# Keys loaded head dimension first, their parts written straight into place; queries loaded to both halves of the partitions

## The chip, the cores and the metric

The kernel runs on one core of a Trainium2 chip. The metric is the device time of one execution in microseconds (us), taken as the median of several runs. The core has five engines that run side by side, each through its own list of instructions, in the order in which the program wrote it: TensorE (PE, matrix products), VectorE (DVE), ScalarE (ACT), GpSimd (POOL) and SyncE (SP). SP and ACT also issue the DMA transfers here.

## The reference, cut to what matters

Attention of 4 batches, 8 heads, 768 positions and head dimension 64 is followed by a bilinear feed-forward layer. The positions form 24 blocks of 32. A query block sees its neighbours, the first and the last block, and three sampled blocks; the first and the last query block see all.

```python
scores = scale * np.matmul(q, k.transpose(0, 1, 3, 2))
mask = np.abs(blk_i - blk_j) <= window
mask = mask | (blk_i == 0) | (blk_j == 0) | (blk_i == n_blocks - 1) | (blk_j == n_blocks - 1)
for qb in range(n_blocks):
    for kb in sampled_blocks[qb]:
        mask[qb * block:(qb + 1) * block, kb * block:(kb + 1) * block] = True
scores = np.where(mask, scores, -1000000000.0)
attn = exp(scores - max) / (sum + 1e-09)
attn_out = np.matmul(attn, v)
x = attn_out.transpose(0, 2, 1, 3).reshape(B * S, H * D)
return ((x @ w_a) * (x @ w_b)) @ w_out
```

The weights are 512 by 1536 (`w_a`, `w_b`) and 1536 by 512 (`w_out`) and reach the chip as 64-bit floats.

## The kernel before

To keep the accuracy of 32 bits on a 16-bit array, each operand is scaled by a power of two and split into a high part (the value in float16) and a low part (what is left, in float16). The second product of the feed-forward layer uses 32-bit parts instead.

**Keys.** `keys(b, g)` loads the keys of two heads of batch `b` (group `g` of four) as 128 positions by 768 numbers (L471). ACT takes the largest absolute value (L481), POOL reduces it over the partitions (L370), DVE makes a scale of it in three small operations (L373, L376, L379). ACT writes the high part (L486), DVE the low part beside it (L487), both into a tile `ks`, of which there are three, shared with the value passes. Positions now lie on the partitions, but the product needs the head dimension there, so SP issues a DMA transpose of `ks` into `keysT` (L495): high part on partitions 0 to 63, low part on 64 to 127. `keysT[1]` and the raw-key buffers serve as landing place for the weights until all of these are unpacked (`w_freed`), and `keysT[b % 2]` is used in turn by the batches (`k_free`).

**Queries.** `queries(cc)` loads 256 positions of all heads, head dimension on partitions 0 to 63 (L633), takes the largest value (L641), and writes the high part (L646, ACT) and the low part (L648, DVE). SP then copies each part to the other half of the partitions (L672, two copies a chunk), so that `QT[:, 0]` holds high over low and `QT[:, 1]` low over high. A product of `QT[:, 0]` and of `QT[:, 1]` with a key column then adds all four combinations.

**Attention of a block (a "unit").** POOL gathers the 8 key blocks into `KG` (L572 to L577); PE writes the mask (L857) and the scores (L756); DVE takes maxima (L872, L875); ACT exponentiates (L882); DVE or ACT write the high part of the probabilities `hl` (L777 or L774) and DVE the low part (L781); SP transposes `hl` to `pt` by DMA (L904); SP loads the value rows `VG` (L607 to L612) from a copy of the split values in DRAM (`vd`, written at L531); PE multiplies (L800); ACT and DVE split the result into `xT` (L1044, L1047). The first and last block take the same way over all keys (L959, L974, L999).

**Feed-forward.** Per chunk of 256 positions: 12 first products `ab` (L1082, 24 matmuls each), ACT and DVE multiply them (L1114, L1117) and split the result (L1139, L1142), and PE makes the second products (L1170 to L1172). The weights are unpacked by DVE from the 64-bit words (L703, L706, L709, three operations a tile), measured and split (L723, L730, L731, L736, L737), interleaved with the attention of the first batch. The second chunk's products are parked in DRAM (L1120) and read back (L1133).

**What sets the order.** All of this is written as flows (Python generators) that ask for an engine, a duration and a rank. `Plan.run` simulates the engines and the DMA with these durations and issues the instruction that could start earliest, weighed by rank. So a changed step changes the order of all engines' lists. The lists are then fixed: an instruction that waits holds up everything behind it on its engine.

Of the kernel before, what the change touches and what calls it, by code (L numbers as in the profile page):

```python
# [224 lines left out]
def act(ns, fn):  # L225
    return [Way("ACT", ns, fn)]
# [16 lines left out]
def kernel(  # L243
# [83 lines left out]
    k_ready = [Event(NG) for _ in range(B)]  # L327
# [5 lines left out]
    q_ready = [Event(3) for _ in range(NC)]  # L333
# [49 lines left out]
    def make_tables():  # L383
# [14 lines left out]
        def load():  # L398
            nc.scalar.dma_start(
                one.rearrange("p a b -> p (a b)"),  # L400
                sampled_blocks.bitcast(I32).rearrange("(o a) b -> o (a b)", o=1),
            )
            nc.scalar.dma_start(
                sb.rearrange("p a b -> p (a b)"), sampled_blocks.bitcast(I32)
            )
            nc.scalar.dma_start(cb, c_blocks)

        yield [Way("ACT", 300, load, 250)]
# [59 lines left out]
    def keys(b, g):  # L468
        yield from gate(first_of[b] - GATE_KV)
        raw, freed = yield from raw_tile(b, g, 0)  # L470
        yield load_way(1000, lambda: nc.scalar.dma_start(raw, k[b, g]))  # L471
        if g + 1 < NG:
            plan.start(keys(b, g + 1), first_of[b] - LEAD_K)
        elif b > 0:
            plan.start(values(b, 0), first_of[b] - LEAD_V)
        t = raw.rearrange("p (t d) -> p t d", d=D)
        done = yield from take("ks", KS_BUFS)
        ks = work.tile([P, 2 * NT, P], F16, tag="ks", name=f"ks{b}_{g}", bufs=KS_BUFS)
        at = at_k + b * NG + g
        s = scale[:, at : at + 1]  # L480
        yield act(1020, lambda: nc.scalar.activation(  # L481
            ks[:, :, :D], t, AF.Abs, accum_out=bound[:, at : at + 1]
        ))
        end = yield from set_scale(slice(at, at + 1), FLOOR_QK)
        k_scale[b].fire(end)
        yield act(930, lambda: nc.scalar.activation(ks[:, :, :D], t, AF.Copy, scale=s))  # L486
        end = yield dve(1070, lambda: nc.vector.scalar_tensor_tensor(  # L487
            ks[:, :, D:], t, s, ks[:, :, :D], ALU.mult, ALU.subtract
        ))
        freed.fire(end)  # L490
        if b == 1:
            yield w_freed
        if b >= 2:
            yield k_free[b - 2]
        end = yield sp(1700, 2200, lambda: nc.sync.dma_start_transpose(  # L495
            keysT[b % 2][:, 2 * g : 2 * g + 2, :].rearrange("p h (t s) -> p (h t) s", s=P),
            ks.rearrange("p t d -> p (t d)"),
        ))
        done.fire(end)
        k_ready[b].fire(end)  # L500
# [125 lines left out]
    def queries(cc):  # L626
# [6 lines left out]
        yield load_way(1400, lambda: nc.scalar.dma_start(t[:D], q[b, c]))  # L633
        if cc + 1 < NC:
# [5 lines left out]
        high, low_ = QT[cc][:D, 0], QT[cc][:D, 1]  # L640
        yield act(2080, lambda: nc.scalar.activation(  # L641
            high, t[:D], AF.Abs, accum_out=bound[:D, at : at + 1]
        ))
        yield from set_scale(slice(at, at + 1), FLOOR_QK)
        s = scale[:D, at : at + 1]
        end = yield act(1890, lambda: nc.scalar.activation(high, t[:D], AF.Copy, scale=s))  # L646
        plan.start(turn_queries(cc, 0), u0 - LEAD_Q, end)
        end = yield dve(2350, lambda: nc.vector.scalar_tensor_tensor(  # L648
            low_, t[:D], s, high, ALU.mult, ALU.subtract
        ))  # L650
        freed.fire(end)
        plan.start(turn_queries(cc, 1), u0 - LEAD_Q, end)
# [15 lines left out]
        q_ready[cc].fire(end)  # L668

    def turn_queries(cc, a):  # L670

        end = yield sp(650, 700, lambda: nc.sync.dma_start(  # L672
            QT[cc][D:, 1 - a], QT[cc][:D, a]
        ))
        q_ready[cc].fire(end)
# [550 lines left out]
def _laid_out(name, a):  # L1226
# [10 lines left out]
    elif name in ("k", "v"):  # L1237
# [3 lines left out]
        a = a.transpose((0, 1, 4, 2, 3, 5) if name == "k" else (0, 1, 4, 3, 2, 5))  # L1241
# [35 lines left out]
```

## Time and profile before

| | us |
|---|---|
| three runs | 924.38, 928.32, 932.67 |
| median | 928.32 |
| span of the profiled execution | 931.3 |

The profiled execution's own time is not given apart from its span; the span lies 3.0 us above the median and inside the range of the three runs. In the rows of the profile, "busy" is time in which an engine worked, a bracket such as [1.86 <-DMA VG<-vd] is the idle time ahead of an instruction and what ended it, and SPq or ACTq is the engine's own queue of DMA issues. Over the span PE is busy 85%, DVE 63%, ACT 49% and POOL 19%. The page's picture in 40 slices shows PE nearly idle for the first tenth and nearly full in the last fifth:

```profile
PE   0134696689869988899989889899999999999998
DVE  3999998977557866765766665645774735432222
DMA  9969999599687699985766984636764706431000
```

### The profile page before, as it was taken

The page shows a single profiled execution, that of the slowest core. Times are in us where ns is not written, and L with a number is a line of the kernel's source. Part 1 is how long each engine was busy: PE and PEld are TensorE (multiplying, and loading weights), DVE is VectorE, ACT ScalarE, POOL GpSimd, SP SyncE. Part 2 cuts the span into 40 slices and gives each one's busy share as a digit, 9 for nine tenths or more (in the row PEclk, how much of TensorE's full clock was granted, in tenths as well). Part 3 has the DMA queues.
Part 4 walks back from the last instruction along what each step waited for, and adds up shares of the span by engine and source line. Part 5 has one row for each costly group of instructions (what it writes and reads, how often), then busy time and mean ns, then how long its engine had stood idle before and what let it go on. Part 6 is the DMA issues. An engine that isn't in the chain of part 4 may idle for free.

```text
span 931.3 us, 23890 instructions
## 1 busy us (share of the span) xinstructions
PE 788.2 (85%) x9024; PEld 629.5 (68%) x9024; DVE 582.6 (63%) x1603; ACT 454.6 (49%) x1087; POOL 176.3 (19%) x416
## 2 busy tenths in 40 slices
PE   0134696689869988899989889899999999999998
PEld 0123584477647776678777777788777778888886
DVE  3999998977557866765766665645774735432222
ACT  4665665566445556554555464434654433332222
POOL 0550232321013421200332320000441300000000
PEclk9999798899989998999999999999999999999999
DMA  9969999599687699985766984636764706431000
GB/s 249 323 165 255 260 242 249 139 172 244 178 201 163 144 203 188 210 172 131 150 155 165 209 164 141 146 79 152 165 141 120 132 1 149 103 97 47 23 1 23
DMA packets 212222, 145.51 MB, mean 156 GB/s; under 512 B 152841, under 2 KB 180490, under 8 KB 211338
## 3 DMA queue, kind: packets, MB, share of 16 engines
q1 hardware_dynamic: 201280, 106.22, 52.4%
q10 hardware_dynamic: 10826, 37.76, 13.7%
q8 instruction: 71, 1.16, 0.5%
q14 instruction: 45, 0.37, 0.1%
HBM read 87.82 MB, written 14.16 MB: 110 GB/s over the span
## 4 chain that ended last, share of the span: by engine, by line
PE 49%; DMA 20%; DVE 18%; ACT 5%; issue 4%; SPq 3%; POOL 1%; ACTq 0%; POOLq 0%; DVEq 0%
PE ab L1082 26%; DMA pt<-hl 12%; PE o L1170 5%; PE o L1172 5%; PE o L1171 4%; PE av L800 4%; DMA keysT<-ks 4%; DVE hl L781 4%; PE s L756 3%; DVE hl L777 2%; DVE xT L1047 1%; DMA VG<-vd 1%; DVE low L872 1%; ACT sm L882 1%; ACT xT L1044 1%
## 5 line engine op out<-in xcount | busy, mean ns | idle before, releaser
L1082 PE MATMUL ab<-xT,wab 128*128 128x256 f16 x3456 | 412.3, 277 | 7.7 <-DVE xT L1047 3.8
L1082 PEld LDWEIGHTS <-wab 128*128 128x128 f16 x3456 | 333.0, 99 | 81.7 <-issue 40.3
L1170 PE MATMUL o<-woh,gh 128*128 128x512 f32 x288 | 128.3, 445 | 13.5 <-ACT gh L1139 13.3
L1114 ACT ACTIVATE a<-ab,f 128x256 f32<-128x256 f32 x144 | 67.8, 471 | 142.5 <-PE ab L1082 131.7
L1117 DVE TENSOR_TENSOR a<-a,ab 128x256 f32<-128x256 f32 x144 | 60.2, 418 | 122.7 <-ACT a L1114 121.8
L882 ACT ACTIVATE sm<-s,low,cq 128x256 f32<-128x256 f32 x176 | 98.1, 560 | 79.1 <-DVE hl L781 43.6
L800 PE MATMUL av<-pt,VG 128*128 128x64 f16 x2688 | 105.7, 196 | 33.9 <-DMA VG<-vd 20.4
L800 PEld LDWEIGHTS <-VG 128*128 128x128 f16 x2688 | 96.3, 100 | 53.2 <-issue 38.5
L1172 PE MATMUL o<-woh,gl 128*128 128x512 f32 x288 | 117.1, 407 | 1.6 <-DVE gl L1142 1.6
L1171 PE MATMUL o<-wol,gh 128*128 128x512 f32 x288 | 115.3, 400 | 0.0
L572 POOL COPY KG<-keysT 128x384 int32<-128x384 int32 x88 | 53.4, 607 | 322.6 <-PE s L756 292.8
L781 DVE SCALAR_TENSOR_TENSOR hl<-sm,den,hl 128x256 f16<-128x256 f32 (+1 forms) x208 | 106.1, 517 | 9.8 <-ACT hl L774 7.6
L577 POOL COPY KG<-keysT 128x128 int32 x264 | 98.1, 409 | 41.3 <-POOL KG L572 27.2
L777 DVE TENSOR_SCALAR hl<-sm,den 128x256 f16<-128x256 f32 (+1 forms) x150 | 57.2, 382 | 59.1 <-DMA pt<-hl 59.0
L1139 ACT CAST gh<-a 128x256 fp32r<-128x256 f32 x132 | 53.2, 403 | 64.2 <-DVE a L1117 63.2
L1170 PEld LDWEIGHTS o<-woh,gh 128*128 128x128 f32 x288 | 55.2, 192 | 33.3 <-ACT gh L1139 16.7
L756 PE MATMUL s<-KG,QT 128*32 128x256 f16 x1408 | 61.1, 299 | 19.4 <-POOL KG L577 19.4
L1142 DVE TENSOR_TENSOR gl<-a,gh 128x256 fp32r<-128x256 f32 x132 | 57.5, 436 | 30.8 <-ACT gh L1139 29.2
L1047 DVE SCALAR_TENSOR_TENSOR xT<-av,xT 64x256 f16<-64x256 f32 x96 | 40.4, 421 | 54.5 <-ACT xT L1044 53.4
L857 PE MATMUL s<-mrows,ident 128*32 128x192 bf16 (+1 forms) x352 | 26.1, 285 | 56.2 <-ACT sm L882 29.6
L756 PEld LDWEIGHTS <-QT 128*32 128x32 f16 x1664 | 45.0, 103 | 34.9 <-issue 29.9
L1172 PEld LDWEIGHTS o<-woh,gl 128*128 128x128 f32 x288 | 55.6, 193 | 18.2 <-DVE gl L1142 5.5
(93 smaller groups left out, 744.5 us busy)
## 6 DMA issues: line engine op xcount, KB each, us to landing
VG<-vd SPq DMA_DIRECT2D x284, 64.0 KB, 2.4
VG<-vd SPq DMA_DIRECT2D x88, 192.0 KB, 3.1
VG<-vd SPq DMA_DIRECT2D x32, 384.0 KB, 3.5
q<-in_q_dram ACTq DMA_DIRECT2D x12, 512.0 KB, 5.5
QT<-QT SPq DMA_DIRECT2D x24, 256.0 KB, 3.9
vd<-vs SPq DMA_DIRECT2D x16, 384.0 KB, 4.6
out_dram<-ou SPq DMA_DIRECT2D x24, 256.0 KB, 3.4
stage<-in_k_dram ACTq DMA_DIRECT2D x12, 384.0 KB, 3.7
```

The lines of the kernel that those rows point to most:

```text
L577: nc.gpsimd.tensor_copy(to[:, :, (5 + r) * w : (6 + r) * w], of[:, :, bass.ds(at, w)])
L756: mm(to[h * BLK : (h + 1) * BLK], q_block(cc, i, 4 * hq + h, a), rhs(4 * hq + h), start=(first and a == 0), stop=(a == 1), skip_group_chec ...
L777: Way("DVE", 227 + n * 0.49, lambda: nc.vector.tensor_scalar(hi, sm, over, None, ALU.mult), 0, X_HIGH),
L781: t = yield dve(221 + n * 1.03, lambda: nc.vector.scalar_tensor_tensor(lo, sm, over, hi, ALU.mult, ALU.subtract))
L800: mm(av[:, g, i % 2, :], w, pt[:, y, cols], start=(i % 2 == 0 and g == 0 and first and n + m == 0), stop=(last and n == len(terms) - 1 and ...
L882: t = yield act(750, lambda hq=hq: nc.scalar.activation(sm[:, hq], ps[:, hq], AF.Exp, bias=low[:, at, hq, 0:1], scale=cq[:, cc, hq : hq + ...
L1082: mm(ab[:, i, :], wab[:, f, i, part, kt, :], xc[:, kt, a, :], start=(i == 0 and kt == 0 and part + a == 0), stop=(kt == KT - 1 and a == 1) ...
L1114: yield act(470, lambda: nc.scalar.activation(a_sb, ab[:, 0, :], AF.Copy, scale=fb[:, f : f + 1]))
L1117: t = yield dve(420, lambda: nc.vector.tensor_mul(a_sb, a_sb, ab[:, 1, :]))
L1170: mm(po, gh[:, js], woh[:, f, :], start=(f == 0), stop=False)
L1171: mm(po, gh[:, js], wol[:, f, :], start=False, stop=False)
L1172: mm(po, gl[:, js], woh[:, f, :], start=False, stop=(f == NF - 1))
```

## The change

The host lays the keys out with the head dimension first: a group's tile is now 2 heads by 64 dimensions on the partitions, and 768 positions along each. The scale is made as before, but the absolute pass writes to a spare tile that is free again at once. Then `key_parts(b, g, x)` runs for each of the two heads. The high part is made by ACT or DVE, whichever the planner finds first, from the 64 partitions of the head straight into `keysT`; DVE writes the low part into the other 64 partitions of the same columns. For the first head of a group the high part lies on partitions 0 to 63, for the second on 64 to 127. The DMA transposes are gone. A pass now works on 64 partitions and 768 columns, so there are two where there was one.

The queries are loaded twice, to partitions 0 to 63 and 64 to 127, and the passes run over 128 partitions at the same column count. `QT[:, 0]` is now the high part on both halves, `QT[:, 1]` the low part; the sum over both is the same four combinations. The copies by SP are gone. The three small loads of the block table move from ACT's queue to SP's.

```diff
-    k_ready = [Event(NG) for _ in range(B)]
+    k_ready = [Event(H) for _ in range(B)]
-    q_ready = [Event(3) for _ in range(NC)]
+    q_ready = [Event(2) for _ in range(NC)]
...
-            nc.scalar.dma_start(cb, c_blocks)
+            nc.sync.dma_start(cb, c_blocks)
...
-        yield act(930, lambda: nc.scalar.activation(ks[:, :, :D], t, AF.Copy, scale=s))
-        end = yield dve(1070, lambda: nc.vector.scalar_tensor_tensor(
-            ks[:, :, D:], t, s, ks[:, :, :D], ALU.mult, ALU.subtract
-        ))
-        freed.fire(end)
         if b == 1:
             yield w_freed
         if b >= 2:
             yield k_free[b - 2]
-        end = yield sp(1700, 2200, lambda: nc.sync.dma_start_transpose(
-            keysT[b % 2][:, 2 * g : 2 * g + 2, :].rearrange("p h (t s) -> p (h t) s", s=P),
-            ks.rearrange("p t d -> p (t d)"),
-        ))
-        done.fire(end)
+        left = Event(2)
+        for x in range(2):
+            plan.start(key_parts(b, g, x, raw, at, left, freed), first_of[b] - LEAD_K, end)
+
+    def key_parts(b, g, x, raw, at, left, freed):
+
+        mine, other = slice(64 * x, 64 * x + 64), slice(64 - 64 * x, 128 - 64 * x)
+        to = keysT[b % 2]
+        s = scale[mine, at : at + 1]
+        h = 2 * g + x
+        yield [
+            Way("ACT", 930, lambda: nc.scalar.activation(
+                to[mine, h], raw[mine], AF.Copy, scale=s
+            )),
+            Way("DVE", 600, lambda: nc.vector.tensor_scalar(
+                to[mine, h], raw[mine], s, None, ALU.mult
+            )),
+        ]
+        end = yield dve(1050, lambda: nc.vector.scalar_tensor_tensor(
+            to[other, h], raw[mine], s, to[mine, h], ALU.mult, ALU.subtract
+        ))
...
-        yield load_way(1400, lambda: nc.scalar.dma_start(t[:D], q[b, c]))
+        def load():
+            for half in range(2):
+                nc.scalar.dma_start(t[half * D : (half + 1) * D], q[b, c])
+
+        yield [Way("LOAD", 950, load, 2600, 1)]
...
-    def turn_queries(cc, a):
-
-        end = yield sp(650, 700, lambda: nc.sync.dma_start(
-            QT[cc][D:, 1 - a], QT[cc][:D, a]
-        ))
-        q_ready[cc].fire(end)
```

PE's list has the same matmuls, and at the first product of each feed-forward chunk the same attention stands ahead of it but for one unit in places. What moves is on the other engines.

On DVE at the start of the program, before (L487 writes the low part of a group's keys, L411 is the first operation on the block table):

```order
L373 TENSOR_SCALAR power<-power 128x1
L487 SCALAR_TENSOR_TENSOR ks_0_113<-wab,scale,ks_0_113 128x12x64
L376 TENSOR_SCALAR rscale<-power 128x1
L487 SCALAR_TENSOR_TENSOR ks_1_115<-wab,scale,ks_1_115 128x12x64
L379 RECIPROCAL scale<-rscale 128x1
L487 SCALAR_TENSOR_TENSOR ks_2_117<-wab,scale,ks_2_117 128x12x64
L411 TENSOR_SCALAR mrow<-mrow 1x72
```

On DVE at the same place now (L504 is the high part of one head's keys, L508 its low part, L555 the reduction of the values' bound):

```order
L379 RECIPROCAL scale<-rscale 128x1
L504 TENSOR_SCALAR keysT_77<-wab,scale 64x768 x2
L379 RECIPROCAL scale<-rscale 128x1
L504 TENSOR_SCALAR keysT_77<-wab,scale 64x768
L508 SCALAR_TENSOR_TENSOR keysT_77<-wab,scale,keysT_77 64x768 x6
L555 TENSOR_REDUCE bound<-bound_v 128x1
L373 TENSOR_SCALAR power<-power 128x1
L411 TENSOR_SCALAR mrow<-mrow 1x72
```

All eight low parts and five of the eight high parts now stand on DVE ahead of the table; ACT has the other three high parts.

On ACT at the start, before (L506 loads values, L486 is a group's high part, L633 loads the first chunk of queries, L399 the table):

```order
L506 DMA wab<-in_v_dram 128x768
L486 ACTIVATE ks_0_113<-wab,scale 128x12x64
L506 DMA wab<-in_v_dram 128x768
L486 ACTIVATE ks_1_115<-wab,scale 128x12x64
L633 DMA q_109<-in_q_dram 64x2048
L486 ACTIVATE ks_2_117<-wab,scale 128x12x64
L399 DMA mrow<-in_sampled_blocks_dram 1x144
```

On ACT at the same place now (L520 loads values, L479 is the keys' absolute pass, L528 the values', L650 loads the queries):

```order
L520 DMA wab<-in_v_dram 128x768
L479 ACTIVATE ks_3_120,bound<-wab 128x768
L520 DMA wab<-in_v_dram 128x768
L528 ACTIVATE va_0_123,bound_v<-wab 128x768
L650 DMA q_109<-in_q_dram 64x2048 x2
L528 ACTIVATE va_1_128,bound_v<-wab 128x768
L528 ACTIVATE va_2_135,bound_v<-wab 128x768
```

The queries' load, now two transfers, stands behind the first value's absolute pass instead of behind the second key's high part.

On SP where the keys of the second batch (b = 1) are made, before (L904 turns probabilities, L1120 parks a product, L495 turns keys, L607 begins the value rows of a unit):

```order
L904 DMA_TRANSPOSE pt_2645<-hl_2601 128x8x128
L1120 DMA parked_g<-a_0_2583 128x256
L495 DMA_TRANSPOSE keysT_78<-ks_0_2501 128x12x128
L1120 DMA parked_g<-a_1_2640 128x256
L495 DMA_TRANSPOSE keysT_78<-ks_1_2515 128x12x128
L1120 DMA parked_g<-a_2_2700 128x256
L1120 DMA parked_g<-a_3_2736 128x256
L495 DMA_TRANSPOSE keysT_78<-ks_2_2517 128x12x128
L495 DMA_TRANSPOSE keysT_78<-ks_3_2675 128x12x128
L607 DMA VG_86<-vd_79 96x1024
```

On SP at the same place now (L1131 parks, L915 turns probabilities, L621 begins the value rows):

```order
L1131 DMA parked_g<-a_0_2583 128x256
L915 DMA_TRANSPOSE pt_2659<-hl_2593 128x8x128
L1131 DMA parked_g<-a_1_2632 128x256
L1131 DMA parked_g<-a_2_2694 128x256
L621 DMA VG_86<-vd_79 96x1024
L566 TENSOR_LOAD offs
```

Nothing of the keys stands ahead of the value rows any more. In exchange 8 low parts and 3 high parts stand within 22 rows of DVE's list there (5 high parts are on ACT), where 4 low parts stood within 27. Over the whole program DVE has 32 low parts of keys where it had 16, 19 high parts of keys where it had none, and 122 high parts of probabilities where it had 150; ACT has 86 of these where it had 58, and 13 high parts of keys where it had 16.

More of the change, by code (lines that the diff above doesn't have):

```diff
@@ L398, in load @@
         def load():
-            nc.scalar.dma_start(
+            nc.sync.dma_start(
                 one.rearrange("p a b -> p (a b)"),
@@ L402, in load @@
             )
-            nc.scalar.dma_start(
+            nc.sync.dma_start(
                 sb.rearrange("p a b -> p (a b)"), sampled_blocks.bitcast(I32)
             )
-            nc.scalar.dma_start(cb, c_blocks)
-        yield [Way("ACT", 300, load, 250)]
+            nc.sync.dma_start(cb, c_blocks)
+        yield [Way("SP", 1425, load, 250, 1)]
         def starts():
@@ L475, in keys @@
             plan.start(values(b, 0), first_of[b] - LEAD_V)
-        t = raw.rearrange("p (t d) -> p t d", d=D)
         done = yield from take("ks", KS_BUFS)
-        ks = work.tile([P, 2 * NT, P], F16, tag="ks", name=f"ks{b}_{g}", bufs=KS_BUFS)
+        spare = work.tile([P, 2 * NT, P], F16, tag="ks", name=f"ks{b}_{g}", bufs=KS_BUFS)
         at = at_k + b * NG + g
-        s = scale[:, at : at + 1]
-        yield act(1020, lambda: nc.scalar.activation(
-            ks[:, :, :D], t, AF.Abs, accum_out=bound[:, at : at + 1]
+        end = yield act(1020, lambda: nc.scalar.activation(
+            spare[:, :NT].rearrange("p t d -> p (t d)"), raw, AF.Abs,
+            accum_out=bound[:, at : at + 1],
         ))
+        done.fire(end)
         end = yield from set_scale(slice(at, at + 1), FLOOR_QK)
         k_scale[b].fire(end)
-        yield act(930, lambda: nc.scalar.activation(ks[:, :, :D], t, AF.Copy, scale=s))
-        end = yield dve(1070, lambda: nc.vector.scalar_tensor_tensor(
-            ks[:, :, D:], t, s, ks[:, :, :D], ALU.mult, ALU.subtract
-        ))
-        freed.fire(end)
         if b == 1:
@@ L494, in keys @@
             yield k_free[b - 2]
-        end = yield sp(1700, 2200, lambda: nc.sync.dma_start_transpose(
-            keysT[b % 2][:, 2 * g : 2 * g + 2, :].rearrange("p h (t s) -> p (h t) s", s=P),
-            ks.rearrange("p t d -> p (t d)"),
-        ))
-        done.fire(end)
+        left = Event(2)
[16 more added lines that the diff above has]
+            to[other, h], raw[mine], s, to[mine, h], ALU.mult, ALU.subtract
+        ))
+        left.fire(end)
+        if left.count == 0:
+            freed.fire(left.at)
         k_ready[b].fire(end)
@@ L639, in queries @@
         QT[cc] = work.tile([P, 2, H, CH], F16, tag="QT", name=f"QT{cc}", bufs=QT_BUFS)
-        high, low_ = QT[cc][:D, 0], QT[cc][:D, 1]
+        high, low_ = QT[cc][:, 0], QT[cc][:, 1]
         yield act(2080, lambda: nc.scalar.activation(
-            high, t[:D], AF.Abs, accum_out=bound[:D, at : at + 1]
+            high, t, AF.Abs, accum_out=bound[:, at : at + 1]
         ))
         yield from set_scale(slice(at, at + 1), FLOOR_QK)
-        s = scale[:D, at : at + 1]
-        end = yield act(1890, lambda: nc.scalar.activation(high, t[:D], AF.Copy, scale=s))
-        plan.start(turn_queries(cc, 0), u0 - LEAD_Q, end)
+        s = scale[:, at : at + 1]
+        yield act(1890, lambda: nc.scalar.activation(high, t, AF.Copy, scale=s))
         end = yield dve(2350, lambda: nc.vector.scalar_tensor_tensor(
-            low_, t[:D], s, high, ALU.mult, ALU.subtract
+            low_, t, s, high, ALU.mult, ALU.subtract
         ))
         freed.fire(end)
-        plan.start(turn_queries(cc, 1), u0 - LEAD_Q, end)
+        q_ready[cc].fire(end)
         yield k_scale[b]
@@ L1240, in _laid_out @@
         a = a.reshape(B, H // 2, 2, S // P, P, D)
-        a = a.transpose((0, 1, 4, 2, 3, 5) if name == "k" else (0, 1, 4, 3, 2, 5))
+        a = a.transpose((0, 1, 2, 5, 3, 4) if name == "k" else (0, 1, 4, 3, 2, 5))
         a = a.reshape(B, H // 2, P, -1)
```

## The prediction, made before the changed kernel was run

> **What bounds the kernel now.** I read the page's engine line first, then busy times in stretches cut at events that the change touches, then the list of waits, then the engines' timelines in the stretches that looked short of work for PE. In the stretches the columns are width, busy us (instructions) of each engine, granted clock, DMA share, GB/s.
>
> ```profile
> PE 788.2 (85%) x9024; PEld 629.5 (68%) x9024; DVE 582.6 (63%) x1603; ACT 454.6 (49%) x1087; POOL 176.3 (19%) x416
> core 0: us, PE busy (x) PEld busy (x) DVE busy (x) ACT busy (x) POOL busy (x), PEclk, DMA share, GB/s
> 0.00:39.74 39.74, 1.56 (x24) 1.18 (x25) 24.00 (x73) 22.50 (x39) 8.44 (x20) 1.00 1.02 269
> 39.74:104.68 64.94, 25.02 (x402) 17.56 (x402) 62.08 (x160) 38.60 (x87) 23.43 (x50) 0.94 0.91 234
> 104.68:186.20 81.52, 65.86 (x724) 50.35 (x724) 75.75 (x201) 49.45 (x119) 25.35 (x41) 0.90 0.86 220
> 186.20:274.60 88.40, 75.67 (x821) 58.36 (x821) 57.17 (x164) 49.97 (x115) 11.35 (x33) 0.94 0.91 203
> 331.00:400.00 69.00, 62.10 (x692) 49.30 (x693) 45.05 (x128) 39.97 (x94) 15.16 (x38) 0.90 0.96 203
> 530.00:610.00 80.00, 71.48 (x806) 57.92 (x807) 47.32 (x133) 41.77 (x93) 10.26 (x28) 1.00 0.66 150
> 610.00:931.00 321.00, 310.56 (x3260) 254.36 (x3260) 144.74 (x387) 114.13 (x293) 32.22 (x81) 1.00 0.38 87
> ```
>
> The kernel is two programs. From 610 us on PE is busy 310.56 of 321 us: nothing but PE work can shorten that, and the change leaves PE's work alone. In front of 39.74 us (the first maximum of scores) PE has 1.56 us of work. From there to 104.68 us (the first feed-forward product that runs without a pause) DVE is busy 62.08 of 64.94 us, and up to 186.2 us still 75.75 of 81.52: DVE is the bound there, and a microsecond less of it, or an earlier start, moves everything behind. Between 186 and 610 us neither is full; PE loses 13 us of 88 in one stretch, 7 of 69 and 9 of 80 in two others. Since PE's list keeps its matmuls and nearly its order, the time after the change is PE's work plus its idle time, and only the idle time can change.
>
> Columns of the waits: us in total, times, longest.
>
> ```profile
> DVE hl L777 <- DMA pt<-hl: 59.0, 37, 5.4
> ACT va L514 <- DMA keysT<-ks: 8.6, 3, 4.8
> PE av L800 <- DMA VG<-vd: 20.4, 14, 3.5
> PE av L800 <- DMA pt<-hl: 8.3, 4, 4.8
> ```
>
> PE itself waits 28.7 us for transfers that SP issues; the keys' transposes hold ACT directly for 8.6 us.
>
> **The change part by part: the start.** Rows of five engines' timelines (start, duration):
>
> ```profile
> 5.03 0.36 POOL L370 PARTITION_ALL_REDUCE power<-bound  x1 [4.60 <-ACT ks L481]
> 5.80 0.16 DVE L379 RECIPROCAL scale<-rscale 128x1 f32<-128x1 f32 x1
> 7.97 0.53 ACTq L633 DMA_DIRECT2D q<-in_q_dram  x1
> 9.86 8.24 SPq L495 DMA_TRANSPOSE keysT<-ks  x3
> 15.49 1.91 ACT L641 ACTIVATE QT<-q 64x2048 f16<-64x2048 f32 x1 [3.57 <-DMA q<-in_q_dram]
> 22.61 1.99 ACT L646 ACTIVATE QT<-q,scale 64x2048 f16<-64x2048 f32 x1
> 25.30 2.34 DVE L648 SCALAR_TENSOR_TENSOR QT<-q,scale,QT 64x2048 f16<-64x2048 f32 x1
> 28.49 0.46 DVE L659 TENSOR_SCALAR cq<-rscale 64x2 f32<-64x2 f32 x2
> 28.60 1.45 SPq L495 DMA_TRANSPOSE keysT<-ks  x1
> 33.97 1.22 POOL L572 COPY KG<-keysT 128x384 int32<-128x384 int32 x1 [2.76 <-DMA keysT<-ks]
> 38.30 1.05 PE L756 MATMUL s<-KG,QT 128*32 128x256 f16 x16 [17.05 <-POOL KG L577]
> 39.74 0.67 DVE L872 TENSOR_REDUCE low<-s 128x2 f32<-128x512 f32 x1
> 104.68 3.71 PE L1082 MATMUL ab<-xT,wab 128*128 128x256 f16 x22 [0.67 <-DVE xT L1047]
> ```
>
> The first scores wait for the last key transpose, issued at 28.60 because it stood behind the queries in SP's list and its group was late on ACT. POOL starts at 33.97 and takes 4.3 us to 38.30. The prices of the new passes come from these groups (columns: busy us, mean ns):
>
> ```profile
> L487 DVE SCALAR_TENSOR_TENSOR ks<-stage,scale,ks 128x768 f16<-128x768 f32 x12 | 12.2, 1023 | 1.0 <-DMA VG<-vd 0.5 <-ACT ks L486 0.4
> L486 ACT ACTIVATE ks<-stage,scale 128x768 f16<-128x768 f32 x12 | 11.1, 932 | 6.4 <-DVE scale L379 6.4
> L777 DVE TENSOR_SCALAR hl<-sm,den 128x256 f16<-128x256 f32 x134 | 50.6, 379 | 57.3 <-DMA pt<-hl 57.1
> L777 DVE TENSOR_SCALAR hl<-sm,den 128x384 f16<-128x384 f32 x16 | 6.6, 413 | 1.9 <-DMA pt<-hl 1.9
> L774 ACT ACTIVATE hl<-sm,den 128x256 f16<-128x256 f32 x42 | 21.1, 503 | 20.6 <-DMA pt<-hl 11.4 <-DVE rscale L376 2.7 <-issue 2.6
> L709 DVE SCALAR_TENSOR_TENSOR w<-stage,w 128x512 int32<-128x512 int32 x10 | 6.8, 693 | 0.0
> L703 DVE TENSOR_SCALAR w<-stage 128x512 int32<-128x512 int32 x10 | 4.4, 443 | 0.0
> q10 hardware_dynamic: 10826, 37.76, 13.7%
> q<-in_q_dram ACTq DMA_DIRECT2D x12, 512.0 KB, 5.5
> stage<-in_moe_w_a_dram ACTq DMA_DIRECT2D x6, 512.0 KB, 4.8
> ```
>
> A low part of one head has as many columns as a group's had before, so I take the same 1.02 us, on half the partitions, twice as often. No row shows a DVE copy of 768 columns: by the slope between 256 and 384 columns (0.034 us for 128) it would take 0.413 + 3 x 0.034 = 0.52, by the ratio 2 x 0.413 = 0.83; I take 0.60, nearer the slope, since short rows carry a fixed part. That a write to the other half of the partitions costs more is shown nowhere; I take nothing, with the range's upper end for it.
>
> Keys: the first scale is there at 5.96. DVE then has 8 x 1.02 + 5 x 0.60 + 12 scale operations of 0.16 = 13.1 us, so the keys are in place at about 20, not at 33.97. The queries then come last. As many ACT passes stand ahead of their load as before, five, but the fifth now needs a value tile, so I put its issue at 10 instead of 7.97 (an estimate). It took 7.5 us before; the second load adds its share of the queue: q10 moved 37.76 MB in 13.7% of 931.3 = 127.6 us, so 0.52 MB takes 1.8. That is 19.3. Behind it stand the absolute pass 1.91, reduction and scale 0.93 (5.03 to 5.96) with some 0.4 for hand-overs, high part 1.99, low part 2.34, factor 0.46: 27.3, in place of the 38.30 at which scores start. In DVE's list three value low parts (3.1) and two weight operations (1.4) stand between the queries' low part and the first maximum, so that comes at about 31.3 instead of 39.74: 8.4 us earlier. From there to the eighth `xT` part, which frees the first product, DVE's list holds four more weight unpackings (4 x (0.443 + 2 x 0.693) = 7.3), three value parts less (3.1) and six high parts of probabilities less (2.3, they go to ACT): 1.9 more. The start gains 6.5 us. Bounds: 10.8 if only the scores' start counted, and a loss of 0.7 if DVE filled every gap (its whole list ahead of that point is 0.7 longer: +4.1 and +3.0 for keys, -1.8, -1.5, -0.7 and -2.3 for weights and probabilities that moved behind it). Cover for the moved weights is that DVE has reached the same count of them (36) by the end of the next chunk in both lists.
>
> The queries' rows above also tell whether two half loads cost two loads: 512 KB on 64 partitions took 5.5 us, 512 KB of weights on 128 partitions 4.8, so half the partitions don't mean half the speed, and my sum counts the second load in full. The Trainium skill, page "DMA: Bandwidth & Descriptors", section "Rules for kernel authors", speaks against the new load: two transfers to disjoint partition halves serialize, since both spread over all 16 DMA engines. By it the time is the 918 below; if the halves ran side by side it would be 1.8 us less, 916.
>
> **The second batch's keys.** Rows of SP, ACT, DVE and PE:
>
> ```profile
> 200.80 9.39 SPq L495 DMA_TRANSPOSE keysT<-ks  x2
> 207.93 0.84 ACT L514 ACTIVATE va<-stage 128x768 f16<-128x768 f32 x1 [4.81 <-DMA keysT<-ks]
> 209.44 0.17 DVE L887 TENSOR_SCALAR den<-den 128x2 f32<-128x2 f32 x1 [4.60 <-ACT sm L882]
> 209.46 0.35 PE L857 MATMUL s<-mrows,ident 128*32 128x192 bf16 x4 [2.64 <-ACT sm L882]
> ```
>
> ACT's value pass waits 4.81 us for a `ks` buffer that a transpose still reads; the exponentials stand behind it, DVE waits for them, and PE for both. Afterwards the absolute pass frees that buffer at once. What SP did behind its 9.39 us, the value rows of the next unit, comes earlier. Against this, between the first feed-forward product and 274.6 us DVE gets 7.7 us more: +4.1 and +1.8 for keys, +4.0 and +0.5 for the work that moved behind, -2.7 for probabilities; its idle time there is 5.8 + 31.2 us, most of it behind 186. I take a gain of 4, near the 4.81 of the wait; bounds -9.4 (all that SP spent) and +5 (7.7 of work less PE's 2.64).
>
> **The other two batches.** DVE gets the rest of +16.3 for the whole program (16 x 1.02 + 19 x 0.60 - 28 x 0.38, less one output copy of about 0.7 that goes to ACT), so 7.9 more, and ACT 12 (28 x 0.50 - 3 x 0.93, and that copy). In the two stretches quoted DVE is idle 24.0 of 69 and 32.7 of 80 us, ACT more: they cover it. SP loses eight transposes and most of 24 query copies. If the cover is gone, the probabilities are late next, and `pt` and PE behind them. I take 0, bounds -4 and +7.9. The 12 further query issues on ACT's queue (0.53 each) and the table's loads on SP cost nothing where ACT is idle half the span.
>
> Sum: 931.3 - 6.5 - 4 + 0 = 920.8 against the profiled span. That span lies 3.0 above the median of 928.3, so the forecast for the median is 918.
>
> **The rivals.** *The start gives nothing (926).* DVE is the bound up to 186 us, so an earlier first score may only turn DVE's early idle into later waits: all 16 issues for the first two units' value rows now stand in SP's list ahead of the first transpose of probabilities, and only three `hl` buffers exist. DVE's waits on `pt` (59.0) speak for it; against it, in that stretch DVE waited just 2.9 us in all. With 1 left at the start and 1 at the second batch: 931.3 - 2 - 3.0 = 926.
>
> *Every DVE microsecond counts (944).* If DVE's list sets the pace everywhere, the start loses 0.7 and the rest 15.6: 931.3 + 16.3 - 3.0 = 944.6. It decides from the point where more than the gains of 10.5 us show on the path. The 22 dense rows at the second batch speak for it, the 31 idle microseconds there against it.
>
> *Transfers were the wait (908).* With 16 transposes and 24 copies off SP's queue, PE's 28.7 us of waiting for `VG` and `pt` may shrink. A third of it, 9.6, gone on top: 908. For it speaks a DMA share of 0.91 to 0.96 in three stretches; against it, the doubled query loads put back the bytes of the copies.
>
> **How the numbers follow.** Forecast (918, own range 912 to 925) 0.52, transfers 0.16, nothing at the start 0.22, DVE the bound 0.10. A measurement tells about 1% from no change, 919.0 to 937.6. A little over half of the forecast's share lies below 919: faster 0.16 + 0.32 = 0.48; same 0.20 + 0.22 = 0.42; slower 0.10. The range 904 to 930 takes in the transfers' case with 4 us to spare and the no-gain case likewise, and leaves out the slower one and tails of 0.08 at most.
>
> **What would show it.** Right: first scores near 27, first maximum near 31, the first product near 98; no wait of ACT for keys; DVE busy near 599, ACT near 467; key rows on 64 partitions of 1.02 us and copies near 0.60. Wrong: the queries landing after 22; a pause of DVE for `pt` of more than 3 us ahead of the first product; PE's idle time in the three middle stretches above the 28 us of before; low parts well over 1.02.

## The result, and the profile after

| | us, median | runs | lowest to highest |
|---|---|---|---|
| before | 930.6 | 18 | 924.2 to 939.6 |
| after | 937.6 | 18 | 930.0 to 947.0 |

The change costs time, somewhat under 1%: the ratio is 1.008, with a 95% interval of 1.005 to 1.011. The forecast was 918, with a range up to 930. It had the wrong sign.

Ratios leave out slow runs (more than 1.5% above the fastest of the same kernel), and the execution that was profiled with this result was one (946.0 us), so places are read from a second profile of the same kernel, which is the first experiment below. Its run took 932.4 us, the lowest of its ten, so it shows a good execution: what an average one loses beyond it is looked for in the experiments.

The page's line of busy times in that second profile:

```profile
PE 783.2 (84%) x9024; PEld 626.2 (67%) x9024; DVE 602.3 (65%) x1609; ACT 463.9 (50%) x1113; POOL 177.8 (19%) x416
```

The same stretches as the prediction quoted of before (columns as there), from the same profile:

```profile
39.74:104.68 64.94, 26.07 (x382) 18.52 (x382) 57.80 (x151) 39.18 (x96) 20.53 (x38) 0.71 0.96 225
104.68:186.20 81.52, 64.83 (x732) 50.54 (x731) 74.93 (x199) 49.52 (x119) 21.35 (x40) 0.94 0.83 208
186.20:274.60 88.40, 76.50 (x884) 59.62 (x887) 67.94 (x179) 54.37 (x128) 16.16 (x36) 0.96 0.79 189
331.00:400.00 69.00, 60.22 (x716) 48.08 (x715) 53.78 (x143) 41.35 (x98) 16.99 (x41) 0.98 0.93 201
530.00:610.00 80.00, 75.44 (x813) 61.31 (x811) 47.68 (x129) 39.24 (x86) 9.07 (x26) 1.00 0.55 130
```

DVE has 20 us more work, as the sum had it (599 forecast, 602.3 here). In the three middle stretches PE is idle for 11.9, 8.8 and 4.6 us, together less than before (12.7, 6.9 and 8.5). The granted clock from 39.74 to 104.68 us is 0.71 in place of 0.94; it is not what sets the first product's time, since two profiles of one experiment below (the small load) had 0.93 and 0.73 there and group 0 of the products at 100.9 and 101.1 us.

The start of the same profile, rows of ACT, DVE, PE and SP in order of time:

```profile
16.94 1.91 ACT L660 ACTIVATE QT<-q 128x2048 f16<-128x2048 f32 x1 [1.93 <-DMA q<-in_q_dram]
26.21 0.83 PE L767 MATMUL s<-KG,QT 128*32 128x256 f16 x12 [1.75 <-DVE QT L666]
31.51 1.27 DVE L883 TENSOR_REDUCE low<-s 128x2 f32<-128x512 f32 x2
33.31 1.91 ACT L660 ACTIVATE QT<-q 128x2048 f16<-128x2048 f32 x1 [2.74 <-DMA q<-in_q_dram]
37.82 0.35 PE L868 MATMUL s<-mrows,ident 128*32 128x192 bf16 x4 [9.75 <-ACT sm L893]
42.85 0.34 SPq L621 DMA_DIRECT2D VG<-vd  x1
43.66 0.61 DVE L792 SCALAR_TENSOR_TENSOR hl<-sm,den,hl 128x256 f16<-128x256 f32 x1
49.99 1.33 SPq L626 DMA_DIRECT2D VG<-vd  x3
51.42 6.34 SPq L915 DMA_TRANSPOSE pt<-hl  x3
57.50 0.35 DVE L788 TENSOR_SCALAR hl<-sm,den 128x256 f16<-128x256 f32 x1 [4.00 <-DMA pt<-hl]
101.44 2.93 PE L1093 MATMUL ab<-xT,wab 128*128 128x256 f16 x13 [0.43 <-DVE xT L1058]
```

The scores come at 26.2 and the first maximum at 31.5, 8.2 us earlier than before. The first product comes at 101.4 (the row is cut off at 104 us), only 3.2 earlier. Between the two DVE has no more work than before, 62.3 us against 62.1, but it is idle for 7.6 us instead of 2.9: what is lost of the gain is lost in waits. The longest is the 4.00 us for a transpose. The first unit's probabilities are split at 44.3 (the DVE row at 43.66), but SP issues the value rows of two units from 42.85 to 51.3 and reaches the first transpose at 51.42. Before, it stood at nearly the same time:

```profile
52.92 1.97 SPq L904 DMA_TRANSPOSE pt<-hl  x1
```

### The profile page after: what moved, and what is told of

It reads as the page before. It is cut to its first block, busy times and chain, and to the rows that moved or that the text cites. A ratio compares the mean times of both kernels' runs of the same rounds, so it can differ in the third digit from the quotient of the medians.

```text
span 944.2 us, 23867 instructions
## 1 busy us (share of the span) xinstructions
PE 791.1 (84%) x9024; PEld 631.1 (67%) x9024; DVE 601.5 (64%) x1609; ACT 464.1 (49%) x1113; POOL 174.7 (19%) x416
## 2 busy tenths in 40 slices
DMA packets 186174, 139.20 MB, mean 147 GB/s; under 512 B 127562, under 2 KB 155211, under 8 KB 184523
## 3 DMA queue, kind: packets, MB, share of 16 engines
q10 hardware_dynamic: 11712, 44.05, 16.4%
## 4 chain that ended last, share of the span: by engine, by line
PE 50%; DMA 20%; DVE 18%; ACT 5%; issue 4%; SPq 2%; ACTq 0%; POOL 0%; DVEq 0%
PE ab L1093 27%; DMA pt<-hl 12%; PE o L1181 5%; PE av L811 5%; PE o L1183 5%; PE o L1182 5%; DMA q<-in_q_dram 3%; DVE hl L792 3%; PE s L767 2%; DMA VG<-vd 2%; DMA u<-parked_g 2%; DVE xT L1058 2%; DVE keysT L508 2%; DVE hl L788 1%; DVE low L883 1%
## 5 line engine op out<-in xcount | busy, mean ns | idle before, releaser
L1093 PE MATMUL ab<-xT,wab 128*128 128x256 f16 x3456 | 416.6, 279 | 19.4 <-ACT wab L741 7.0
L591 POOL COPY KG<-keysT 128x128 int32 x264 | 95.0, 399 | 34.8 <-POOL KG L586 25.8
L788 DVE TENSOR_SCALAR hl<-sm,den 128x256 f16<-128x256 f32 (+1 forms) x122 | 46.1, 378 | 60.7 <-DMA pt<-hl 60.4
L370 POOL PARTITION_ALL_REDUCE power<-bound x44 | 23.6, 538 | 241.0 <-ACT QT L660 136.5
L1055 ACT ACTIVATE xT<-av 64x256 f16<-64x256 f32 x96 | 36.2, 377 | 58.2 <-PE av L811 33.8
```

The source lines that it names most:

```text
L591: nc.gpsimd.tensor_copy(to[:, :, (5 + r) * w : (6 + r) * w], of[:, :, bass.ds(at, w)])
L1093: mm(ab[:, i, :], wab[:, f, i, part, kt, :], xc[:, kt, a, :], start=(i == 0 and kt == 0 and part + a == 0), stop=(kt == KT - 1 and a == 1) ...
```

## Experiments

Two mechanisms were put against each other first: the *burst theory* (the second query load makes transposes beside it land late) and the *DVE theory* (the keys' extra work on DVE delays the probabilities). A third was that every list of instructions is a draw of its own (*order theory*). Ratios below are to runs of before that were taken together with the kernel in question, with their 95% intervals.

**The changed kernel again**, with no edit.

> The changed kernel as it stands, for a second profile of it. Burst theory (the second query load of 512 KB makes a transpose of probabilities that is issued beside it land late, 9 to 13 us in place of 3.6, and PE waits): the two long waits of the first profile, PE for pt at 306 us (8.75) and PE for gh at 406 us (3.94), come back at the same two query loads, within 3 us of their size; time about 937. DVE theory (the 16 us more that DVE has of the keys delay the probabilities): PE idle time is spread over many short waits and those two are not the same again. Chance theory (that run alone was bad): both waits are gone and the time is about 930.

940.1 us over ten runs, ratio 1.006 (1.002 to 1.009). In the profile one long wait is smaller (PE for `pt` at 297 us: 3.88 instead of 8.75) and the other is gone; this execution took 932.4 us, about as much as before. So the long waits come and go from run to run. The nine other runs took 933.2 to 943.7 us; what they waited for was not profiled. None of the three expectations is met as written.

**The two parts alone.** For the keys alone, `queries` is that of before:

```diff
-            for half in range(2):
-                nc.scalar.dma_start(t[half * D : (half + 1) * D], q[b, c])
+        yield load_way(1400, lambda: nc.scalar.dma_start(t[:D], q[b, c]))
...
+        plan.start(turn_queries(cc, 0), u0 - LEAD_Q, end)
```

> Keys in the new layout, queries as before: one load to 64 partitions and copies to the other half on SP. Burst theory: the loss goes with the second load, and the gains of the keys stay (4 at the second batch, and a part of the 3 seen at the start): 922 to 927. DVE theory: DVE keeps its 16 us more and SP gets its copies back: 937 or more. Order theory (the list of instructions of each variant is another draw, worth 5 us either way): anywhere from 925 to 940, and nothing that follows from the parts.

941.2 us, 1.007 (1.003 to 1.011). The burst theory's figure is missed by 14 us: without a second load this kernel is no faster. The DVE theory's "937 or more" is met.

For the queries alone, `keys` is that of before, with its transposes on SP.

> Queries loaded twice, keys as before with transposes on SP. Burst theory: the loss without the gains, 934 to 940, with PE waits for pt beside query loads. DVE theory: no extra DVE work for keys, so no loss: 926 to 930. Order theory: as for the keys alone, 925 to 940, with no bond to the parts.

964.8 us, 1.033 (1.028 to 1.038), worse than any theory had it. The first product is at 118.5 us, 15 later than before: the first keys' transposes took 13.92 us on SP beside the doubled load, where they had taken 8.24, and the tables' loads stand behind them on SP, so that the mask is there at 35 us. The parts don't add: +0.7% and +3.3% alone, +0.6 to 0.8% together.

**The second load's bytes, with every list left as it is.** This edit separates bytes from order (a fixed tile for the queries, and one fill of its upper half on POOL, are left out here):

```diff
-            for half in range(2):
-                nc.scalar.dma_start(t[half * D : (half + 1) * D], q[b, c])
+            nc.scalar.dma_start(t[:D], q[b, c])
+            nc.scalar.dma_start(t[D:, 0], q[b, c, :, 0])
```

> The changed kernel with the second query load cut to one head of eight (64 KB in place of 512); the other heads of the upper half hold a fill, so that part of the scores is left out. Every instruction stands where it stood (one fill on POOL at the start is added), so the work of DVE and every order are those of the changed kernel. Burst theory: transposes and value rows issued beside query loads land in 4 to 6 us, the wait for VG at 669 to 684 us (2.75 and 3.98 in the two profiles) goes below 1.5, and the time is 926 to 931. DVE theory and order theory: within 2 us of the changed kernel, 936 to 941.

921.7 us, 0.985 (0.979 to 0.990). The same with real values in the upper half:

> As the small second load, but the first chunk of queries is loaded in full to both halves, so that the upper half holds real queries of the first chunk from then on (seven heads of eight stay old, and that part of the scores is left out). If the missing bytes made the 921.7 us: 921 to 927. If the constant fill made it: 934 to 940.

920.0 us, 0.988 (0.982 to 0.995). So the fill is not the reason: 448 KB less in each of twelve loads (eleven in the second run) take 18 to 20 us off the 940.1, or 16 to 20 by the ratios, and leave 1.2 to 1.5% less than before. The time of the packets on q10, the queue of ACT's transfers, falls by 23 us (16.9% of 930.6 is 157, 14.6% of 918.6 is 134); its rows in the second profile of the changed kernel and in that of the small load:

```profile
q10 hardware_dynamic: 11712, 44.05, 16.9%
q10 hardware_dynamic: 11712, 38.54, 14.6%
```

The other direction, before with the load added:

```diff
-        yield load_way(1400, lambda: nc.scalar.dma_start(t[:D], q[b, c]))
+        def load():
+            for half in range(2):
+                nc.scalar.dma_start(t[half * D : (half + 1) * D], q[b, c])
+
+        yield load_way(1400, load)
```

> The kernel before with a second 512 KB load of the same queries beside each query load, to the upper 64 partitions, where nothing reads it. Every list stays as it was, but for the 12 further issues on the ACT queue. Burst theory (the second load in flight beside transposes of probabilities and value rows is the loss, 10 to 17 us by the run with the small second load): 942 to 951. Order theory: before stays where it is, 931 to 936.

962.4 us, 1.026 (1.020 to 1.033): 28 us, in lists that were made without that load. And the queries alone, without the bytes:

> Queries alone (keys as before with transposes; 965 us) with the second load cut to one head of eight from the second chunk on, so that part of the scores is left out. If the bytes of the second load are the loss there too: 930 to 948. If its lists or the lack of the new keys are: 958 to 966.

940.5 us, 1.010 (1.007 to 1.014): 24 us less than with them. In three sets of lists much the same bytes cost 18 to 28 us.

Where it goes shows in the start of chosen groups of 24 first products (us, from the records of `ab` on PE in one profile of each; group 0 begins with two matmuls some 1 us ahead of the first product that runs without a pause):

| group | before | after, again | small load | before plus load |
|---|---|---|---|---|
| 0 | 103.4 | 100.4 | 100.9 | 110.3 |
| 24 | 273.7 | 267.6 | 264.0 | 288.2 |
| 48 | 427.2 | 421.5 | 415.8 | 448.9 |
| 78 | 606.4 | 597.6 | 590.7 | 633.0 |
| 102 | 740.5 | 739.9 | 727.8 | 768.5 |
| 143 | 921.7 | 920.8 | 908.7 | 950.6 |

Even the good execution of the changed kernel loses 12 us to the one with the small load: 3.6 by group 24, 3.3 more by group 78, and 5.2 between 78 and 102, where the last query load stands (661 us). Against before, this execution is 8.8 us ahead at group 78 and only 0.6 at group 102. Nearly all of that goes in one stretch, from the last query load to group 102, here before and in the second profile of the changed kernel:

```profile
669.40:740.50 71.10, 66.29 (x900) 53.75 (x896) 43.96 (x128) 35.44 (x94) 20.64 (x53) 1.00 0.67 138
661.10:739.90 78.80, 69.37 (x920) 55.52 (x916) 47.70 (x136) 35.34 (x97) 22.04 (x57) 0.96 0.60 129
```

PE is idle for 9.4 us of it instead of 4.8, and at a lower granted clock it is busy for 69.37 instead of 66.29. The mean share of the transfers hides the place: in the ten us from 661 it is 0.98, with PE busy for 6.0. With the small load the whole way from 78 to 102 takes 137.0 us, still 2.9 more than before, so some of the loss there is not the bytes. Two of the stretches in the profile of the small load:

```profile
186.20:274.60 88.40, 78.52 (x906) 60.95 (x904) 68.39 (x181) 54.41 (x130) 18.50 (x42) 0.94 0.78 185
530.00:610.00 80.00, 76.92 (x786) 62.51 (x785) 45.59 (x120) 35.45 (x83) 7.50 (x18) 1.00 0.44 106
```

PE does 78.52 and 76.92 us of work where the changed kernel did 76.50 and 75.44, and in the later one the transfers' share is 0.44 instead of 0.55. (The counts differ too, 786 matmuls against 813 in the later one: the faster kernel is further on, at other work.) The rows of PE, ACT and SP at the last query load, in the second profile of the changed kernel:

```profile
660.48 2.46 SPq L626 DMA_DIRECT2D VG<-vd  x3
661.07 0.47 ACTq L650 DMA_DIRECT2D q<-in_q_dram  x1
661.58 0.86 ACTq L650 DMA_DIRECT2D q<-in_q_dram  x1
663.38 1.27 SPq L915 DMA_TRANSPOSE pt<-hl  x1
669.24 1.28 PE L811 MATMUL av<-pt,VG 128*128 128x64 f16 x21 [3.98 <-DMA VG<-vd]
```

The value rows and the transpose are issued beside the pair of loads; PE waits 3.98 us for them.

**DVE's work.** The low part as a plain copy, in the same place of every list:

```diff
-        end = yield dve(1050, lambda: nc.vector.scalar_tensor_tensor(
-            to[other, h], raw[mine], s, to[mine, h], ALU.mult, ALU.subtract
+        end = yield dve(1050, lambda: nc.vector.tensor_scalar(
+            to[other, h], raw[mine], s, None, ALU.mult
```

> The changed kernel with the low part of each head of keys taken by a plain scaled copy (0.60 us) instead of the scaled subtraction (1.02), so that the low part of the keys is left out of the scores. DVE has 32 x 0.42 = 13.4 us less; every order stays. DVE theory (the 16 us more of DVE are the loss): 926 to 931, and the time between the first product and the end of the first batch of work near 270 us shrinks by 4 or more. Burst theory and order theory: within 3 us of the changed kernel, 935 to 941.

947.4 us, 1.012 (1.006 to 1.018): DVE is busy 590.4 us instead of 602.3, and the kernel is slower. From group 0 to group 24, where the DVE theory wanted 4 us less, its profile has 168.8 us instead of 167.2; most of its loss lies from there to group 48 (168.2 us instead of 153.9), where the wait shown next falls. The DVE theory is not borne out. What its profile shows in place of a gain, first in rows of SP, ACT and PE:

```profile
294.38 2.12 SPq L915 DMA_TRANSPOSE pt<-hl  x1
294.49 1.29 ACTq L650 DMA_DIRECT2D q<-in_q_dram  x2
300.79 1.25 SPq L915 DMA_TRANSPOSE pt<-hl  x1
310.86 1.50 PE L811 MATMUL av<-pt,VG 128*128 128x64 f16 x24 [11.69 <-DMA VG<-vd]
```

and then in two stretches, just ahead of the meeting and in it:

```profile
296.00:298.00 2.00, 2.00 (x31) 1.46 (x30) 0.74 (x3) 0.70 (x2) 0.31 (x2) 1.00 0.88 208
299.00:307.00 8.00, 0.17 (x1) 0.10 (x1) 0.00 (x0) 0.00 (x0) 0.65 (x3) 0.72 1.07 69
```

A transpose and the pair of loads are issued within 0.1 us. From 299 to 307 us the transfers' engines are full (share 1.07) but move 69 GB/s, the compute engines all but stand still, and PE waits 11.69 us. The second load landed 15.7 us after its issue, the transpose of 300.79 after 11.6. Stretches of the second profile of the changed kernel, with the same pair of loads and a transpose issued 1.0 us behind it:

```profile
290.00:295.00 5.00, 3.38 (x37) 2.35 (x35) 0.85 (x3) 0.74 (x2) 1.54 (x6) 1.00 1.00 218
295.00:299.00 4.00, 1.73 (x27) 1.56 (x27) 1.72 (x5) 0.25 (x1) 0.00 (x0) 0.60 1.17 228
```

218 and 228 GB/s at much the same share. Before plus the second load has another meeting at 400 us, in rows of ACT, SP and PE:

```profile
400.03 0.48 ACTq L635 DMA_DIRECT2D q<-in_q_dram  x1
400.44 2.59 SPq L908 DMA_TRANSPOSE pt<-hl  x1
400.55 1.65 ACTq L635 DMA_DIRECT2D q<-in_q_dram  x1
414.92 0.51 ACT L778 ACTIVATE hl<-sm,den 128x256 f16<-128x256 f32 x1 [10.03 <-DMA pt<-hl]
415.77 0.80 PE L1174 MATMUL o<-woh,gh 128*128 128x512 f32 x1 [9.18 <-ACT gh L1143]
```

The transpose and the second load both land some 14.5 us after their issue; ACT stands for 10.03 us until a buffer that the transpose reads comes free, and PE waits for the work behind that on ACT. The Trainium skill says, in "DMA: Bandwidth & Descriptors", section "Rules for kernel authors", that a transpose next to ordinary DMAs needs nothing. That is said beside the rule that two transposes must not run at once, for the sake of the data, and no time is given; these rows show that such a meeting can take long. In the other direction, a transpose can also be late without a query load in flight: in the profile of the spaced pieces below, one that was issued at 109.1 us took 11.4.

**The lists themselves.** One figure of the planner moved by 10 ns (`DMA_AHEAD` 1750 to 1760), in before and after:

> The kernel before with one of the planner figures moved by 10 ns (how far a transfer may be issued ahead of the queue, 1750 to 1760): the same work, in lists that differ from the old ones in many places. Order theory: the time moves by several us though no work changed, and since the lists of before were the ones that its figures were set for, upward: 935 to 942. Burst theory and DVE theory: what sets the time is work and bytes, so 929 to 934.

> The changed kernel with the same planner figure moved by 10 ns. Order theory: several us from 938 in either direction, 928 to 946. Burst theory and DVE theory: 936 to 941.

Before: 937.2 us, 1.005 (1.000 to 1.009). After: four runs from 949.1 to 970.3, with a median of 966.2; no ratio is given, and only the lowest is used here. So 10 ns in a plan move the time by about half a per cent in one kernel and, by that single run, by about 1% in the other. With the small load in the nudged lists:

> The changed kernel with the nudged planner figure (966 us) and with the second query load cut to one head of eight, so that part of the scores is left out. Burst theory: what the nudge cost is that two query loads now meet transposes (PE waits of 11.57 and 9.58 us at 169 and 424 us); without the bytes both shrink below 4 and the time is 930 to 945. Order theory: the list itself is the cost, 958 to 968.

926.0 us, 0.993 (0.990 to 0.997): 23 us below that one run. With the small load the nudge costs 4 us (921.7 to 926.0), with the full load 9 by that run (940.1 to 949.1): about half of what it cost went with the bytes of the query loads. The same nudge to the keys alone:

> Keys alone (941 us) with the planner figure moved by 10 ns. If the 941 was bad luck of its lists: 922 to 935. If the work of the keys on DVE costs what the transposes saved: 938 to 945.

933.4 us, 0.998 (0.994 to 1.002) instead of 1.007. The keys alone gain nothing that can be told from their lists.

**Ways around the load.** Smaller pieces (the query tile's rows two words longer, so that the transfers' queue shows 22,464 packets instead of 11,712):

> The changed kernel with rows of the query tile two words longer, so that the transfer writes pieces of 1 KB in place of rows of 8 KB: the same bytes and the same lists. If large pieces hold up the small ones of a transpose beside them, the long landings (a transpose of 9 to 14 us, a second load of 13 to 16) go and the time is 925 to 932. If bytes in flight alone count, 936 to 941. If more pieces make the load itself slower, above 941.

941.2 us, 1.006 (1.003 to 1.009). No transpose in the profile that could be followed took over 9.9 us, but the time stayed. That the pieces took away the worst meetings is not shown, since the second profile of the changed kernel, with the large ones, had none over 8.5 us either. The loads on the transposes' own queue (`nc.sync` for `nc.scalar`), for all chunks and then from the third on:

> The changed kernel with both query loads issued by SP, on the queue that also carries the transposes, instead of ACT; every list stays but for these 24 issues. If two queues that mix slow each other down: no transpose or load takes over 10 us, transposes behind a load land in up to 9, and the time is 925 to 933. If the bytes alone are the cost: 936 to 942. If a transpose behind 1 MB in its own queue is worse than beside it: above 943.

> The changed kernel with the query loads on SP, the queue of the transposes, from the third chunk on; the first two stay on ACT. It should keep the first product near 100 us, where all loads on SP had 104.8, and lose no more than those behind it: 926 to 931. If the queue made no difference: 936 to 941.

933.2 us, 1.004 (1.000 to 1.008), and 933.8, 1.003 (1.000 to 1.006). The twelve runs of the first lie within 6.7 us, where the changed kernel's ten lay within 11.3, and of the transposes that could be followed none took over 7.0 us in the one profile. The intervals overlap with the changed kernel's, so that the gain of some 0.3% is likely and not certain. Four pieces spaced by the plan:

```diff
+        for x in range(4):
+            yield [Way("LOAD", 950, lambda x=x: load(slice(2 * x, 2 * x + 2)), 650, 1)]
+            if x < 3 and cc >= 2:
+                yield 2000
```

> The changed kernel with the query load in four pieces of two heads (256 KB each, for both halves), each planned 2 us after the one before has landed from the third chunk on. Its lists are new. If it is the length of a burst that makes a transpose beside it land late: no transpose over 9 us, 920 to 932. If the bytes alone are the cost: 935 to 945.

933.7 us, 0.997 (0.993 to 1.001), in lists of its own. The time lies between the two that were expected, and three transposes of its profile took 10.4 to 13.3 us, so the shorter pieces did not keep them short. One load, and the upper half by copies on POOL from the third chunk on:

```diff
+            end = yield pool(900, lambda hs=hs: nc.gpsimd.tensor_copy(
+                QT[cc][D:, a, hs].bitcast(I32), QT[cc][:D, a, hs].bitcast(I32)
+            ))
```

> The changed kernel, but from the third chunk of queries on they are loaded once, and the upper half of the partitions is filled by copies on POOL (four of 64 x 512 words per chunk, about 0.8 us each by the key copies of 128 x 384 at 0.63); the first two chunks, which meet no transposes, are loaded twice. Burst theory: 920 to 930. Order theory (its lists are new): anywhere from 928 to 950.

> Copies on POOL (940 us) with the planner figure moved by 10 ns. If the 940 was bad luck of its lists: 920 to 933. If the copies on POOL themselves cost it (40 x 1.03 us ahead of key copies): 937 to 945.

940.1 us, 1.004 (1.000 to 1.008), and 935.1, 0.998 (0.995 to 1.002). The copies take 1.03 us each, not 0.8. Of the kernels that do the whole computation none has an interval that lies below before.

## Why the prediction was wrong, point by point

**Most prices were right.** Scores 26.2 (27.3 forecast), first maximum 31.5 (31.3), low parts 1.02 to 1.04 us (1.02), copies 0.62 (0.60), DVE 602.3 (599), ACT 463.9 (467). ACT's wait for the keys' transposes is gone. Part of the good fit of the scores is luck: the first queries landed at 16.9 instead of 19.3, and their scale was there only 4.0 us behind that, where the sum had 3.2.

**The step that failed** is the one sentence that the query issues "cost nothing where ACT is idle half the span". It priced the twelve loads as issues on ACT's queue. As transfers they were priced once, 1.8 us at the start, though the same working gave 1.8 for each: twelve make 21.6 us. The runs with and without those bytes differ by 18 to 20 us, so nearly all of it lay on the path. The rows for it were quoted: a share of the transfers of 0.86 to 1.02 up to 274 us and 0.96 from 331 to 400. In these runs a gap on the engine that issues a transfer was no cover for it. The view of the end of the kernel was too narrow with it: from 610 us on nothing but PE's work could shorten the time, but waits could lengthen it, and behind the last query load the lead of 8.8 us shrank to 0.6.

**The halves don't run side by side.** The second load of the first two pairs landed 1.9 and 2.3 us behind the first, near the 1.8 of the sum; with 64 KB in the second it was 0.2 and 0.3 us. The Trainium skill's rule in the prediction ("DMA: Bandwidth & Descriptors", section "Rules for kernel authors") has it so, and the trace agrees.

**The rest of the sum held better than its result.** Without the bytes the gain is 9.6 us at 273.7, where the start and the second batch together were to give 10.5, and 13 at the end. The kernel with the small load ran in 921.7 and 920.0 us, near the 918 to which the sum came. That is in part luck: its start gave 2.5 of the 6.5, the way to group 24 then 7.1 where 4 was forecast, and the keys alone, without any second load, gained nothing (1.007 and 0.998).

**The start (6.5 forecast, 3.2 measured)** was mis-sized in the way that its rival described: the value rows ahead of the first transposes on SP. With the first maximum 8.2 us earlier, the first transpose is 1.5 earlier. That is read from the trace; a list with the transposes ahead was not tried. Their place is not the whole of it: in the profile of the small load the first transpose stands at 48.92, another 2.5 us earlier, DVE then waits 7.03 us for one, and group 0 still comes at 100.9. For the same reason the bytes of the second load are not what holds the start.

**Only PE's idle time can change** was not exact. Its matmuls were the same, yet its busy time was 788.2 us before, 793.7 with the load added to before, 783.2 and 775.7 in the second profile and in the small load with real values. The mean granted clock of these profiles (0.968, 0.941, 0.961 and 0.969) goes with it in the first two only. In places the rows show more: scores ahead of the wait at the last query load, and behind it (the second row is cut off at 671 us, after half of its matmuls):

```profile
664.46 0.61 PE L767 MATMUL s<-KG,QT 128*32 128x256 f16 x16
670.58 0.64 PE L767 MATMUL s<-KG,QT 128*32 128x256 f16 x8
```

Eight matmuls take as long as sixteen did, with a mean granted clock of 0.84 from 661 to 671 us, so that this wait of 3.98 us cost more than its length. The Trainium skill names a cause ("TensorE: Matmul & The Clock Gate", Part 1: the clock gate follows how busy the array has been lately); the rows agree.

**The rivals.** *Every DVE microsecond counts* had the right sign and a time too high by 6 (944 against 937.6), for a reason that is not borne out: with 12 us less of DVE's work the kernel was not faster. *Transfers were the wait* had the right resource and the wrong sign; the objection to it, that the doubled loads put back the bytes of the copies, was the case, although all bytes together fell from 145.51 to 139.20 MB. Nor does every transfer lie on the path. On q1, the queue of SP's transfers, before and in the second profile of the changed kernel:

```profile
q1 hardware_dynamic: 201280, 106.22, 52.4%
q1 hardware_dynamic: 174346, 93.63, 45.5%
```

That is 488 us of packets' time against 423: the removed transposes and copies took 65 us, q10 gained 30, and the time did not fall.

**The signs.** The pause of DVE ahead of the first product was there (4.00 us, more than 3). The three middle stretches had less idle time than before and so said "right" in a kernel that was slower: they were cut at the old times, and the later losses fell outside them.

What stays open: how much of the lasting difference to before is the list of each kernel. Two lists of one kernel differ by up to 1%, which is as much as the change itself. Open too is why the time that left SP's queue was worth so little, while the bytes added on ACT's queue were paid nearly in full.

## What to carry to other kernels

Price a transfer that is loaded twice in the time of the transfers' queues, for every repeat of it, and look at the transfers' share in the few microseconds where it stands: in the second profile of the changed kernel the mean from 598 to 740 us was 0.54, in the ten us behind the last query load 0.98. That the issuing engine was idle hid nothing here. When a planner makes the order, compare two versions with the order held (the same lists, fewer bytes) before believing a difference under 1%, since a nudge of 10 ns moves as much. A start that comes earlier is worth only what the queues behind it let through: look at what stands there ahead of the first instruction that is now ready.

## What the hardware showed that was not expected

Behind a transpose on one queue and 1 MB of loads on another, issued within 0.1 us, the moved bytes fell to 69 GB/s for 8 us with the transfers' engines full, against 218 to 228 in one place where the transpose came 1.0 us later. The landing times were 11.6 us for a transpose and 15.7 for the second load, against medians of 3.6 for the transposes that could be followed and 7.1 for the loads. With pieces of 1 KB, or with the loads on the transposes' queue, no transpose that could be followed took over 9.9 or 7.0 us; these are single profiles, and one of the changed kernel itself had none over 8.5. Why the rate falls was not found.
